# Reloads for a weight check moved to unit 80 and after, and a planner's order made anew with other task times

## The chip, the cores and the metric

One NeuronCore of a Trainium2 chip runs the whole kernel. The metric is the device time of one execution in microseconds; less is better. PE is TensorE's matmul, PEld its weight load, DVE VectorE, ACT ScalarE, POOL GpSimd, SP the engine that here only issues DMAs. A trailing q marks an engine's sequencer.

## What is computed

A decayed linear attention over 4 x 8 heads of 768 steps, and then a gated two-layer block over its 3072 rows of 384 numbers:

```python
for t in range(S):
    state = alpha[:, :, t, :, None] * state + einsum('bhd,bhe->bhde', k[:, :, t], v[:, :, t])
    y[:, :, t] = einsum('bhd,bhde->bhe', q[:, :, t], state)
h = x @ w_in                       # x: y as 3072 rows of 384; w_in 384 x 2048, float64
sp = where(h > 20, h, log1p(exp(min(h, 20))))
return ((h * tanh(sp)) @ w_out)    # w_out 2048 x 384, float64
```

## The kernel before

**Pieces of work.** The attention is cut into 24 chunks (`attention(n)`), each 64 steps of one pair of batches. The gated block is cut into units (`unit`): `SEGMENTS` lists 105 of them, each a slice of 128 of the 2048 inner columns (f = 0 to 15) for 2 or 4 chunks of 128 rows. The weights are 16 slices of 768 KB (`weight(f)`).

**A weight slice** is loaded by SP into one of two `stage` buffers (L426), taken apart by four DVE operations through the one `lead` buffer (L441, L447, L453, and L468, which stands on PE and ACT for f < 3) and one ACT copy (L459). The units' matmuls read the two halves in `wio`.

**A chunk** costs DVE two scans (L570, L583), a reciprocal, two products (L579, L593), a decay (L601), two masks (L650), and later a state update (L800) and the lower halves of x (L699). PE turns k (L761), makes scores (L616 and L639) and y with the change of state (L616, L680). Six small DMAs of x (`move`, L720) then go out on SP; the chunk's units can begin when they have landed. Three `qka` buffers hold loaded chunks.

**A unit** is nine matmuls up into one of two `h` banks (L826), then ACT exp, square, log, exp; a DVE gate (L847); an ACT copy (L853); a DVE lower half (L856); and three matmuls down for each of its chunks (L885). Sums of up to four chunks stay in banks o0 to o3 over many units; chunks 0 to 3 and 4 to 7 use the same four. So units 24 to 33 (chunks 0 to 3, f = 6 to 15) have to end before a down of units 34 to 40 (chunks 4 to 7, f = 9 to 15) can begin. `EARLY_BANKS` says which banks a chunk uses; without an entry it is "att" thrice.

**The check.** Each weight slice is loaded a second time (`weight_check`, L497) into a `stage` buffer, and one DVE operation (L506 or L508) gathers its exponents in `unlike`; `weights_checked` (L519, L520) looks at them. At the end flags are summed (L1003), every engine loads the result (L1141) and branches (L1142): `general_path` is the other arm, not run with these inputs. In the arm that runs, SP goes over the counters of its DMA queues that the other arm would have advanced.

**What sets the order.** The program for each engine is a fixed list. `Plan.order` makes it while the kernel is built: every task has an engine, a cost (`COST`: time on the engine, time until its result), needs, buffers, and a key. Of each engine's tasks it takes the one that can begin first by these costs, and among those that can begin at once the one with the lowest key. The chip then follows the lists at its own pace, with semaphores. Keys count units:
- unit i: i + SHIFT; its downs have that + 3 (`LAG`).
- chunk n: due + SHIFT. Due is 8 units before its first unit (`LEAD`), and at least 2 before the next chunk's due. Scores have + 0.2, y + 0.5, the six moves + 0.64, the load - 6.
- weight f: first unit with f, less 4 (`W_LEAD`), + SHIFT; its load has 4 less.
- check f: `CHECK_FROM` + f x `CHECK_STEP` + SHIFT; its load has 4 less and comes behind the up of one unit (`behind`, a condition for the planner alone).

Where by these costs PE would have nothing to do in the first 130 us, the planner puts in fills (L940): matmuls of a constant into a free bank, whose result nobody reads.

Of the kernel before, what the change touches and what calls it, by code (L numbers as in the profile page):

```python
# [27 lines left out]
B, H, S, D = 4, 8, 768, 48  # L28
DM, FF = 384, 2048
P = 128  # L30
# [4 lines left out]
NFF = FF // P  # L35
NK = DM // P
# [26 lines left out]
FIRST_W = -6.0  # L63
CHECK_FROM = 57.0
CHECK_STEP = 2.7
COLD = 14
# [3 lines left out]
EARLY_BANKS = {  # L70
    0: "o1 o1 att o3 att".split(),
    1: "att o3 o1 att h".split(),
    2: "att h att att o3".split(),
    3: "o0 h att o0 o3".split(),
    4: "o2 att o3".split(),
    9: "o3 att o2".split(),
    10: "o1 o3 att".split(),
    11: "o3 o1 att".split(),
    13: "o1 o2 att".split(),
    14: "att o0 o1".split(),  # L80
    15: "o3 att att".split(),
    16: "att att o1".split(),
    17: "o2 o3 att".split(),
    18: "o3 att o0".split(),
    20: "att o3 o2".split(),
    21: "att att h".split(),
    22: "att o2 att".split(),
}
SHIFT = {
    "chunk": {  # L90
# [4 lines left out]
    },  # L95
    "unit": {
# [17 lines left out]
    },  # L114
    "weight": {
        0: -1.8297, 1: -88.668, 2: -1.298, 3: -0.44909, 4: -0.76088, 5: -0.16277, 7: -7.1065,
        8: -3.6601, 9: -2.0214, 11: 0.91205, 12: -0.61512, 13: 2.8687, 15: 3.8897,
    },
    "weight check": {
        1: 2.9506, 2: -1.2413, 3: -2.7653, 4: -7.2029, 5: -0.37293, 6: -5.1126, 7: -4.9684,  # L120
        8: -0.99544, 9: -8.3869, 10: -8.6038, 11: 6.855, 12: 3.149, 13: -24.555, 14: 0.49888,
        15: 1.0013,
    },
# [26 lines left out]
class Plan:  # L150
# [14 lines left out]
    def add(  # L165
        self, engine, cost, late, key, emit, needs=(), uses=(), behind=(), port=False,
        small=(False, False),
    ):
        t = Task(engine, cost, late, key, emit, port)
        t.small = small  # L170
        t.needs, t.uses, t.behind = list(needs), list(uses), list(behind)
        for u in t.uses:
            u.left += 1
            u.key = min(u.key, key)
        self.tasks.append(t)
        return t
# [107 lines left out]
WINDOW = 10**6  # L284
SAME = 0.155
QUEUE = 8
# [6 lines left out]
    "cold fill": (0.32, 0.36), "fill": (0.1635, 0.2), "off": (0.21, 0.37), "w off": (0.88, 1.06),  # L293
    "w seen": (1.4, 1.6),
    "scan": (1.152, 1.27), "inverse": (0.113, 0.21), "mult k": (0.562, 0.745), "mult": (0.602, 0.725), "half mult": (0.32, 0.46), "check": (0.2, 0.34),
    "state": (0.272, 0.4), "state0": (0.21, 0.35), "decay": (0.469, 0.605), "mask": (0.335, 0.49),
    "scores0": (0.65, 0.77), "scores": (0.91, 1.0), "y0": (1.12, 1.2), "y": (1.36, 1.43),
    "y last": (0.88, 0.99), "turn": (0.34, 0.66),
# [12 lines left out]
for _n in (1, 2):  # L311
    COST["lead", _n] = (0.095 + 0.2 * _n, 0.17 + 0.2 * _n)
    COST["bits", _n] = (0.114 + 0.401 * _n, 0.2 + 0.4 * _n)
    COST["w left", _n] = (0.069 + 0.401 * _n, 0.185 + 0.4 * _n)
    COST["w hi", _n] = (0.095 + 0.32 * _n, 0.21 + 0.32 * _n)
# [4 lines left out]
def fast_path(ctx, tc, qka, v, w, out, good):  # L320
    nc = tc.nc
# [15 lines left out]
    for rows in (slice(0, HALF), slice(HALF, P)):  # L337
        nc.gpsimd.affine_select(
            out=causal_f[rows], in_=one[rows, :HALF], pattern=[[1, HALF]], compare_op=ALU.is_ge,
# [151 lines left out]
    def weight_check(f):  # L491
# [19 lines left out]

        t = add("SP", *COST["load w"], key - 4, load, uses=[again], behind=[ups[int(key)]])
        seen.append(
# [493 lines left out]
def general_path(ctx, tc, q, k, v, alpha, w_in, w_out, out):  # L1007
# [9 lines left out]
    with tc.tile_pool(name="rec", bufs=1) as sb:  # L1017
# [4 lines left out]
        with tc.For_i(0, S, T) as t0:  # L1022
            qt, kt, vt, at = [sb.tile([BH, T, D], F32, name=n) for n in ("qt", "kt", "vt", "at")]
            yt = sb.tile([BH, T, D], F32, name="yt")
            for dst, src in zip((qt, kt, vt, at), flat):
                nc.sync.dma_start(dst, src[:, ds(t0, T), :])
            for t in range(T):
# [7 lines left out]
            for b in range(B):  # L1035
                dst = x_d[b * S : (b + 1) * S, :].rearrange("t (h e) -> h t e", h=H)
                nc.sync.dma_start(dst[:, ds(t0, T), :], yt[b * H : (b + 1) * H])

    with tc.tile_pool(name="conv", bufs=1) as sb:
# [5 lines left out]
        with tc.For_i(0, DM * FF // P, W) as c0:  # L1045
            t = sb.tile([P, 2, W, 2], I32, name="words")
            for m in range(2):
                nc.sync.dma_start(
                    t[:, m].rearrange("p c w -> p (c w)"), words[m][:, ds(c0 * 2, 2 * W)]
                )  # L1050
# [21 lines left out]
            for m in range(2):  # L1072
                nc.sync.dma_start(w_d[m][:, ds(c0, W)], f[:, m])

    with tc.tile_pool(name="moe", bufs=1) as sb, tc.tile_pool(name="pm", bufs=1, space=PSUM) as ps:
# [6 lines left out]
        as_rows = lambda t, n: t.rearrange("p c -> (p c)").rearrange("(s r c) -> r s c", s=n, r=P)  # L1082
        nc.sync.dma_start(wi, as_rows(w_d[0], NK))
        nc.sync.dma_start(wo, as_rows(w_d[1], NFF))
        with tc.For_i(0, B * S, P) as r0:
            x = sb.tile([P, DM], F32, name="x_g")
            nc.sync.dma_start(x, x_d[ds(r0, P), :])
            xT = sb.tile([P, NK, P], F32, name="xT_g")
# [27 lines left out]
            nc.scalar.copy(o, po)  # L1116
            nc.sync.dma_start(out[ds(r0, P), :], o)

# [91 lines left out]
```

## Time and profile before

| | us |
|---|---|
| time, median of 3 runs (480.13 to 480.57) | 480.56 |
| time of the profiled execution | 480.47 |
| its span, first to last instruction | 478.8 |
| around the span | 1.67 |
| PE busy in it, of which fills | 466.8, of which 17.5 |
| DVE busy, ACT busy | 340.9, 365.6 |
[...]

A row of a timeline is: start and length in us, engine, line, operation, written tile and read tiles, their shapes, how often; in brackets the idle time of the engine just before, and what ended it. "issue" there means that the engine waited for nothing that the profile shows. A matmul's length includes its way through the array, so one begins before the last has ended: the pace of a group is read from its start to the start of the next group. DMA shares are of 16 DMA engines; a row of DMA issues ends with the KB of one and the median us from issue to landing, a row of a queue has packets, MB and share. Packets of the kind "instruction" bring the engines' own programs.

### The profile page before, as it was taken

Reading aid. Unit: us, or ns where it says so; the run is one execution under the profiler, and the core shown is the slowest. Engines: PE = TensorE matmul, PEld = TensorE weight load, DVE = VectorE, ACT = ScalarE, POOL = GpSimd, SP = SyncE. Lnnn points to the kernel's source line nnn. Section 1 sums busy time; section 2 is a strip of 40 time slices with the busy share of each in tenths; the row PEclk is TensorE's granted clock in tenths of the full one; section 3 lists DMA queues with packets and bytes.
Section 4 is the critical chain, followed back from the end, with each engine's and each line's share of the span. In section 5 each row is a group of like instructions: output and inputs, shape, how many; then the busy total and the mean of one; then the engine's idle time right before and its main releaser. Section 6 shows DMA issues by size and latency. Waiting matters only on the chain.

```text
span 478.8 us, 12662 instructions
## 1 busy us (share of the span) xinstructions
PE 466.8 (97%) x5233; PEld 418.6 (87%) x5233; DVE 340.9 (71%) x586; ACT 365.6 (76%) x816; POOL 2.4 (1%) x12
## 2 busy tenths in 40 slices
PE   7999999999999999999999989999999999999996
PEld 4668888998989889999999978999989989999995
DVE  8999999999995799789434368797376343355432
ACT  2567879889998968877887846878758878778784
POOL 2000000000000000000000000000000000000000
PEclk9999999999999999999999999999999999999998
DMA  8777536353220363154000266824252000080001
GB/s 292 247 235 253 178 127 231 135 168 115 66 67 9 129 197 111 67 184 159 0 1 0 77 223 213 318 68 132 63 183 81 1 7 4 22 291 18 0 2 70
DMA packets 20078, 56.82 MB, mean 119 GB/s; under 512 B 4016, under 2 KB 12464, under 8 KB 20016
## 3 DMA queue, kind: packets, MB, share of 16 engines
q1 hardware_dynamic: 19872, 55.77, 33.9%
q8 instruction: 42, 0.69, 0.6%
q10 hardware_dynamic: 144, 0.20, 0.1%
q14 instruction: 20, 0.16, 0.1%
HBM read 48.87 MB, written 4.72 MB: 112 GB/s over the span
## 4 chain that ended last, share of the span: by engine, by line
PE 74%; DVE 16%; ACT 6%; issue 2%; DVEq 0%
PE bank L826 31%; PE bank L885 31%; PE bank L616 4%; PE bank L940 2%; DVE t L847 2%; PE bank L639 2%; DVE rest L570 2%; PE bank L761 2%; PE bank L680 2%; DVE g L856 1%; DVE qka L583 1%; DVE w_lead L453 1%; DVE w_lead L447 1%; DVE wio L468 1%; DVE state L800 1%
## 5 line engine op out<-in xcount | busy, mean ns | idle before, releaser
L885 PE MATMUL bank<-wio,g 128*128 128x384 f32 x1152 | 207.4, 329 | 0.0
L826 PE MATMUL bank<-xs,wio 128*128 128x512 f32 (+1 forms) x945 | 205.3, 364 | 1.1 <-DVE t L847 0.8
L885 PEld LDWEIGHTS bank<-wio,g 128*128 128x128 f32 x1152 | 189.8, 189 | 5.0 <-issue 0.2
L826 PEld LDWEIGHTS bank<-xs,wio 128*128 128x128 f32 x945 | 164.0, 189 | 22.1 <-DVE t L847 3.1
L856 DVE SCALAR_TENSOR_TENSOR g<-t,g 128x512 fp32r<-128x512 f32 (+1 forms) x105 | 66.3, 642 | 55.7 <-ACT g L853 55.5
L847 DVE SCALAR_TENSOR_TENSOR t<-t,bank 128x512 f32<-128x512 f32 (+1 forms) x105 | 67.0, 638 | 48.0 <-ACT t L844 47.7
L835 ACT ACTIVATE t<-bank 128x512 f32<-128x512 f32 (+1 forms) x105 | 58.8, 560 | 48.6 <-PE bank L826 45.5
L853 ACT ACTIVATE g<-t 128x512 fp32r<-128x512 f32 (+1 forms) x105 | 60.5, 586 | 20.7 <-DVE t L847 10.6
L841 ACT ACTIVATE t<-t,fifth 128x512 f32<-128x512 f32 (+1 forms) x105 | 71.7, 684 | 2.2
L838 ACT ACTIVATE t<-t 128x512 f32<-128x512 f32 (+1 forms) x105 | 62.0, 592 | 2.1
L844 ACT ACTIVATE t<-t 128x512 f32<-128x512 f32 (+1 forms) x105 | 61.7, 588 | 1.5
L570 DVE TENSOR_TENSOR_SCAN rest<-qka,behind 112x520 f32<-112x520 f32 x24 | 29.7, 1238 | 1.3 <-DMA qka<-in_qka_dram 1.1
L583 DVE TENSOR_TENSOR_SCAN qka<-qka,ahead 112x520 f32<-112x520 f32 x24 | 29.6, 1232 | 0.0
L694 ACT ACTIVATE xs<-bank 112x256 fp32r<-112x256 f32 x48 | 15.8, 379 | 14.8 <-PE bank L680 6.9
L650 DVE COPY_PREDICATED probs<-causal,bank 128x256 f32<-128x256 uint32 x48 | 18.8, 439 | 6.8 <-PE bank L639 5.7
L835 ACT ACTIVATION_READ_ACCUMULATOR t<-bank 128x1 f32 x105 | 20.5, 195 | 0.0
L616 PE MATMUL bank<-qka,state 48*48 48x64 f32 (+1 forms) x704 | 20.0, 221 | 0.3 <-DVE qka L593 0.2
L800 DVE TENSOR_TENSOR state<-bank,state 112x192 f32<-112x192 f32 x40 | 12.9, 353 | 10.3 <-PE bank L680 6.4
L616 PEld LDWEIGHTS bank<-probs,v 64*48 64x48 f32 (+1 forms) x768 | 13.6, 127 | 7.4 <-issue 3.4
L940 PE MATMUL bank<-behind 112*128 112x384 bf16 x76 | 17.5, 367 | 2.4 <-DVE behind L362 2.4
L616 PEld LDWEIGHTS bank<-qka,state 48*48 48x48 f32 (+1 forms) x704 | 15.3, 127 | 4.8 <-issue 3.1
L508 DVE SCALAR_TENSOR_TENSOR unlike<-wc,unlike 128x768 int32<-128x768 int32 x15 | 17.0, 1134 | 3.0 <-DMA wc<-in_wp_dram 3.0
(70 smaller groups left out, 316.6 us busy)
## 6 DMA issues: line engine op xcount, KB each, us to landing
qka<-in_qka_dram SPq DMA_DIRECT2D x22, 772.5 KB, 6.0
ws<-in_wp_dram SPq DMA_DIRECT2D x16, 768.0 KB, 4.4
wc<-in_wp_dram SPq DMA_DIRECT2D x16, 768.0 KB, 5.0
v<-in_vp_dram SPq DMA_DIRECT2D x24, 192.0 KB, 3.2
out_dram<-osb SPq DMA_DIRECT2D x15, 192.0 KB, 2.3
xs<-xs SPq DMA_DIRECT2D x144, 16.0 KB, 3.6
out_dram<-part SPq DMA_DIRECT2D x8, 192.0 KB, 2.5
qka<-in_qka_dram SPq DMA_DIRECT2D x2, 260.5 KB, 3.8
```

Source lines behind the costliest of these rows:

```text
L570: nc.vector.tensor_tensor_scan(t[:, :0:-1], alpha()[:, :0:-1], behind[:, ::-1], 0.0, ALU.mult, ALU.max)
L583: nc.vector.tensor_tensor_scan(a, a, ahead, 0.0, ALU.mult, ALU.max)
L616: return nc.tensor.matmul(summed(x)[HALF * side : HALF * side + wide, j], weights(wide), moving, start=start, stop=stop, skip_group_check= ...
L826: nc.tensor.matmul(p[:, :N], wio[:, z, f, 0, s * P : s * P + P], by_token(x[:, s, :, a]), start=m == 0, stop=m == len(passes) - 1,)
L835: nc.scalar.activation(wide(t), wide(h), AF.Exp, accum_out=uchk[:, at : at + 1])
L838: nc.scalar.activation(wide(t), wide(t), AF.Square, bias=1.0)
L841: nc.scalar.activation(wide(t), wide(t), AF.Ln, bias=fifth, scale=0.2)
L844: nc.scalar.activation(wide(t), wide(t), AF.Exp, scale=-1.0)
L847: nc.vector.scalar_tensor_tensor(wide(t), wide(t), 2.5, wide(h), ALU.subtract, ALU.mult)
L853: nc.scalar.activation(g.tile[:, 0, :N], wide(t), AF.Copy, scale=-0.4)
L856: late[mybir.EngineType.DVE] = nc.vector.scalar_tensor_tensor(g.tile[:, 1, :N], wide(t), -0.4, g.tile[:, 0, :N].bitcast(F32), ALU.mult, AL ...
L885: made = nc.tensor.matmul(o.tile[:, :DM], g.tile[:, a, j * C : (j + 1) * C], spread(wio[:, z, f, 1]), start=begins and m == 0, stop=end an ...
```

## The change

Reloads and checks have their keys from 80 on in steps of 1.05 and no shifts, and each reload comes behind the up of the unit that `CHECK_FROM` + f x `CHECK_STEP` names. All shifts of chunks, units and weights and all early banks are new. Some task times of the planner are new, and `SAME`, by which the planner lets small matmuls follow small ones earlier. In `general_path` all DMAs go from SP's queue to POOL's. No operation on data in the arm that runs is added, removed or resized.

```diff
-CHECK_FROM = 57.0
-CHECK_STEP = 2.7
+CHECK_FROM = 80.0
+CHECK_STEP = 1.05
...
 EARLY_BANKS = {
-    0: "o1 o1 att o3 att".split(),
...
-    16: "att att o1".split(),
-    17: "o2 o3 att".split(),
-    18: "o3 att o0".split(),
-    20: "att o3 o2".split(),
-    21: "att att h".split(),
-    22: "att o2 att".split(),
+    0: "att att o0 att o1".split(),
...
+    17: "o0 att att".split(),
+    18: "o1 o3 o2".split(),
+    19: "o1 att att".split(),
+    21: "att o3 o2".split(),
 }
 SHIFT = {
     "chunk": {
-        0: -15.485, 1: -12.079, 2: -11.416, 3: -11.777, 4: -0.33581, 5: 1.6274, 6: -0.39491,
-        7: 1.5292, 8: -3.7056, 9: -0.21255, 10: 1.4965, 11: -0.0097693, 12: -8.9524, 13: -7.0071,
-        14: -7.7326, 15: -9.7059, 16: -9.893, 17: -7.5153, 18: -6.1157, 19: -3.0825, 20: -3.4548,
-        21: -3.5097, 22: -5.4473, 23: 2.0482,
+        0: -25.301, 1: -20.34, 2: -13.806, 3: -11.23, 4: 4.0517, 5: 4.0522, 6: 1.3752,
+        7: 0.80117, 8: -3.6406, 10: -0.2315, 11: 1.4964, 12: -2.1029, 13: -3.5335, 14: -4.1898,
+        15: -1.3139, 16: -11.016, 17: -10.764, 18: -8.744, 19: -5.913, 20: 0.29965, 21: 0.71137,
+        22: 0.22851, 23: 4.8182,
     },
     "unit": {
...
-        85: -1.3119, 86: -0.71045, 87: -3.9605, 88: 0.03174, 89: -0.96161, 90: -4.4882,
...
-        104: -0.55339,
...
+        79: 2.1935, 80: 0.049234, 81: 1.4386, 82: 0.13712, 83: -0.18346, 85: 1.6807, 86: 0.44438,
+        87: 0.29401, 89: -0.3835, 90: 0.76619, 91: -0.44769, 92: 0.71218, 93: -0.79337,
...
+        100: -0.91033, 101: 0.41587, 102: -0.2893, 104: 11.602,
     },
     "weight": {
-        0: -1.8297, 1: -88.668, 2: -1.298, 3: -0.44909, 4: -0.76088, 5: -0.16277, 7: -7.1065,
-        8: -3.6601, 9: -2.0214, 11: 0.91205, 12: -0.61512, 13: 2.8687, 15: 3.8897,
+        0: 0.44719, 1: -53.48, 2: -19.485, 3: -0.79106, 4: 2.6882, 5: -2.1876, 6: -2.2027,
+        7: 4.5643, 8: 4.1694, 9: 0.97864, 10: -1.3843, 11: -0.13355, 12: -2.0257, 13: -0.16652,
+        14: 6.07, 15: 10.996,
     },
     "weight check": {
-        1: 2.9506, 2: -1.2413, 3: -2.7653, 4: -7.2029, 5: -0.37293, 6: -5.1126, 7: -4.9684,
-        8: -0.99544, 9: -8.3869, 10: -8.6038, 11: 6.855, 12: 3.149, 13: -24.555, 14: 0.49888,
-        15: 1.0013,
+
     },
 }
...
-SAME = 0.155
+SAME = 0.33
...
-    "w seen": (1.4, 1.6),
+    "w seen": (1.6, 1.8),
...
-    "scores0": (0.65, 0.77), "scores": (0.91, 1.0), "y0": (1.12, 1.2), "y": (1.36, 1.43),
+    "scores0": (0.65, 0.77), "scores": (0.91, 1.0), "y0": (1.12, 1.2), "y": (1.39, 1.46),
...
-    COST["lead", _n] = (0.095 + 0.2 * _n, 0.17 + 0.2 * _n)
-    COST["bits", _n] = (0.114 + 0.401 * _n, 0.2 + 0.4 * _n)
+    COST["lead", _n] = (0.095 + 0.24 * _n, 0.17 + 0.24 * _n)
+    COST["bits", _n] = (0.114 + 0.435 * _n, 0.2 + 0.435 * _n)
...
-        t = add("SP", *COST["load w"], key - 4, load, uses=[again], behind=[ups[int(key)]])
+        t = add("SP", *COST["load w"], key - 4, load, uses=[again], behind=[ups[int(CHECK_FROM + f * CHECK_STEP)]])
...
-                nc.sync.dma_start(dst, src[:, ds(t0, T), :])
+                nc.gpsimd.dma_start(dst, src[:, ds(t0, T), :])
...
```

## Rows read from the trace of the kernel before

**Rows 1.** The page: busy us (share of span) and instructions of TensorE, VectorE, ScalarE
```profile
PE 466.8 (97%) x5233; PEld 418.6 (87%) x5233; DVE 340.9 (71%) x586; ACT 365.6 (76%) x816; POOL 2.4 (1%) x12
```
**Rows 2.** Stages: length, then busy us (count) by engine, granted clock, DMA share, GB/s
```profile
60.00:146.00 86.00, 85.08 (x849) 77.25 (x848) 85.28 (x139) 74.61 (x180) 0.00 (x0) 1.00 0.37 126
146.00:268.00 122.00, 121.76 (x1476) 111.59 (x1476) 83.27 (x150) 95.82 (x207) 0.00 (x0) 1.00 0.25 84
268.00:300.00 32.00, 29.72 (x624) 26.05 (x623) 21.25 (x43) 20.41 (x50) 0.00 (x0) 1.00 0.56 201
```
**Rows 3.** The group of fills (page), and DVE alone from its first scan on
```profile
L940 PE MATMUL bank<-behind 112*128 112x384 bf16 x76 | 17.5, 367 | 2.4 <-DVE behind L362 2.4
...
3.68:145.59 141.91, 139.59 (x232) 1.00 0.51 175
```
**Rows 4.** Timelines of DVE and PE where weight slice 15 is finished
```profile
145.59 0.96 DVE L468 TENSOR_TENSOR wio<-w_lead,wio 128x768 fp32r<-128x768 f32 x1 [0.32 <-ACT wio L459]
...
145.97 4.37 PE L826 MATMUL bank<-xs,wio 128*128 128x512 f32 x18
```
**Rows 5.** Timeline of PE at its longest wait; the page's queue of PE's instruction packets
```profile
283.92 0.26 PE L616 MATMUL bank<-probs,v 64*48 64x64 f32 x2 [1.48 <-issue]
...
q8 instruction: 42, 0.69, 0.6%
```
**Rows 6.** DMA in 268 to 278, in 278.5 to 281.5, in 281.5 to 284
```profile
wc<-in_wp_dram SPq DMA_DIRECT2D x2, 768.0 KB, 7.5
...
q1 hardware_dynamic: 221, 1.21, 98.6%
xs<-xs SPq DMA_DIRECT2D x5, 16.0 KB, 5.4
...
q8 instruction: 1, 0.02, 2.4%
```
**Rows 7.** Timeline of PE, 288 to 297: two waits for DVE
```profile
289.00 0.60 PE L761 MATMUL bank<-ident,qka 112*128 112x112 f32 x4 [0.56 <-DVE qka L579]
...
295.26 0.69 PE L616 MATMUL bank<-probs,v 64*48 64x64 f32 x32 [0.21 <-DVE probs L650]
...
296.57 1.24 PE L885 MATMUL bank<-wio,g 128*128 128x384 f32 x6
```
**Rows 8.** The tile wc: ns min/median/max, first and last start
```profile
L508 DVE SCALAR_TENSOR_TENSOR unlike<-wc,unlike x15: 945/1143/1218, 281.0 to 440.7; 128x768 int32<-128x768 int32 x15
```
**Rows 9.** Timeline of PE: attention among units; chunk 23's y and what follows
```profile
161.79 0.69 PE L616 MATMUL bank<-probs,v 64*48 64x64 f32 x32
...
163.82 2.21 PE L826 MATMUL bank<-xs,wio 128*128 128x512 f32 x9
...
385.98 0.46 PE L616 MATMUL bank<-qka,state 48*48 48x64 f32 x16
...
386.83 2.21 PE L826 MATMUL bank<-xs,wio 128*128 128x512 f32 x9
388.97 0.69 PE L616 MATMUL bank<-probs,v 64*48 64x64 f32 x32
...
403.56 2.11 PE L826 MATMUL bank<-xs,wio 128*128 128x512 f32 x9
405.51 2.11 PE L885 MATMUL bank<-wio,g 128*128 128x384 f32 x12
```
**Rows 10.** The tile xs from 384 to 404: chunk 23's six moves and their landing
```profile
L720 SPq DMA_DIRECT2D xs<-xs x6: 507/580/597, 392.1 to 395.4; - x6
...
DMA to landing us min/median/max: 1.8/1.8/2.3
```
**Rows 11.** Timeline of the last units: downs after the last up, and the last DVE operation
```profile
465.84 7.96 PE L885 MATMUL bank<-wio,g 128*128 128x384 f32 x48
...
470.74 0.69 DVE L856 SCALAR_TENSOR_TENSOR g<-t,g 128x512 fp32r<-128x512 f32 x1 [0.76 <-ACT g L853]
```
**Rows 12.** Line 1142, SP's counters after the branch: ns, first and last start
```profile
L1142 SPq EVENT_SEMAPHORE  x8: 17/17/17, 476.4 to 477.4; - x8
```

More of the change, by code (lines that the diff above doesn't have):

```diff
@@ L70 @@
 EARLY_BANKS = {
-    0: "o1 o1 att o3 att".split(),
[L72 to L81, printed above, removed]
-    16: "att att o1".split(),
-    17: "o2 o3 att".split(),
-    18: "o3 att o0".split(),
-    20: "att o3 o2".split(),
-    21: "att att h".split(),
-    22: "att o2 att".split(),
+    0: "att att o0 att o1".split(),
+    1: "o1 h o1 o0 o3".split(),
+    2: "att o3 o0 att h".split(),
+    3: "att o1 att o3 o0".split(),
+    4: "o3 att att".split(),
+    5: "o3 att att".split(),
+    9: "o1 att att".split(),
+    10: "att o3 o2".split(),
+    11: "o3 att att".split(),
+    12: "o2 att o3".split(),
+    13: "att o2 o0".split(),
+    14: "h att att".split(),
+    17: "o0 att att".split(),
+    18: "o1 o3 o2".split(),
+    19: "o1 att att".split(),
+    21: "att o3 o2".split(),
 }
@@ L1036, in general_path @@
                 dst = x_d[b * S : (b + 1) * S, :].rearrange("t (h e) -> h t e", h=H)
-                nc.sync.dma_start(dst[:, ds(t0, T), :], yt[b * H : (b + 1) * H])
+                nc.gpsimd.dma_start(dst[:, ds(t0, T), :], yt[b * H : (b + 1) * H])
     with tc.tile_pool(name="conv", bufs=1) as sb:
@@ L1047, in general_path @@
             for m in range(2):
-                nc.sync.dma_start(
+                nc.gpsimd.dma_start(
                     t[:, m].rearrange("p c w -> p (c w)"), words[m][:, ds(c0 * 2, 2 * W)]
@@ L1072, in general_path @@
             for m in range(2):
-                nc.sync.dma_start(w_d[m][:, ds(c0, W)], f[:, m])
+                nc.gpsimd.dma_start(w_d[m][:, ds(c0, W)], f[:, m])
     with tc.tile_pool(name="moe", bufs=1) as sb, tc.tile_pool(name="pm", bufs=1, space=PSUM) as ps:
@@ L1082, in general_path @@
         as_rows = lambda t, n: t.rearrange("p c -> (p c)").rearrange("(s r c) -> r s c", s=n, r=P)
-        nc.sync.dma_start(wi, as_rows(w_d[0], NK))
-        nc.sync.dma_start(wo, as_rows(w_d[1], NFF))
+        nc.gpsimd.dma_start(wi, as_rows(w_d[0], NK))
+        nc.gpsimd.dma_start(wo, as_rows(w_d[1], NFF))
         with tc.For_i(0, B * S, P) as r0:
             x = sb.tile([P, DM], F32, name="x_g")
-            nc.sync.dma_start(x, x_d[ds(r0, P), :])
+            nc.gpsimd.dma_start(x, x_d[ds(r0, P), :])
             xT = sb.tile([P, NK, P], F32, name="xT_g")
@@ L1116, in general_path @@
             nc.scalar.copy(o, po)
-            nc.sync.dma_start(out[ds(r0, P), :], o)
+            nc.gpsimd.dma_start(out[ds(r0, P), :], o)
 @with_exitstack
```

27 rows, old and new, of the table SHIFT are left out of this document.

## The prediction

> **What bounds the kernel now.** I read the page first: TensorE is busy for 97% of the span [rows 1], so at first sight PE is the bound and only its idle time and its fills can be won. The fills alone take 17.5 us [rows 3]. The table by stage, read next, corrects this. From 60 to 146 us DVE is busy for 85.28 of 86.00 us, and only after 146 does it have room (83.27 of 122.00) while PE has none (121.76) [rows 2]. For DVE alone from its first scan at 3.68 to 145.59 the row says 139.59 busy of 141.91 us, so 2.32 idle [rows 3]. The timelines show where the one bound hands over to the other: DVE begins the last operation on weight slice 15 at 145.59, and PE begins the up of unit 33, the first reader of that slice, at 145.97 [rows 4]. So there are two stages: DVE sets the pace up to 146, PE from there to the end. The fills are the shadow of DVE's stage; they are not won by giving PE other work unless DVE comes to slice 15 sooner.
>
> After 146, PE's losses are few. The timeline has one wait of 1.48 us in the midst of chunk 18's y, ended by nothing that the profile shows ("issue") [rows 5], and two for DVE, 0.56 and 0.21 us, both in chunk 19 [rows 7]. The stage table agrees: from 268 to 300 PE is busy for 29.72 of 32.00 us, where from 146 to 268 it lacks only 0.24 [rows 2].
>
> What was the 1.48 us? The queue q8 brought 42 packets and 0.69 MB, 16 KB a packet [rows 5]. PE had 5233 weight loads and 5233 matmuls [rows 1], some 249 a packet: these are its instruction blocks. Two reloads were issued between 268 and 278 and took 7.5 us to land; from 278.5 to 281.5 the DMA engines were 98.6% taken by q1, the data, and no q8 packet moved; one came between 281.5 and 284 [rows 6], and PE went on at 283.92 [rows 5]. Chunk attention burns instructions: a y with the next chunk's scores begins at 161.79 and is over at 163.82 [rows 9], 128 matmuls in 2.03 us by their count there. I take the wait for one for a block that stood behind loads, the two reloads among them: the first check of their line ran at 281.0 [rows 8].
>
> **The change, part by part.** I start from the profiled execution's own 480.47 us; the median of the runs is 0.09 above.
>
> *Start, to 146.* The work that DVE must do before unit 33 doesn't change: slices 0 to 15, chunks 0 to 8, the units' gates, and the scans of chunks 9 to 11, for their new keys (29.0, 30.8, 34.5: due 29, 31, 33 plus shift) stay below that of slice 15, which goes from 32.9 to 40.0 (unit 33, less 4, plus 10.996). Slices 3 and 5 come before chunk 4 now (1.2 and 1.8 against 3.05), which gives PE the four-chunk units 6 to 8 sooner and may save fills, but what PE gains there it waits for at unit 33. At best DVE's 2.32 us of idle time go [rows 3]. At worst slice 15, whose key now lies behind those of the gates of units 31 to 38, lets two more gates of 0.7 us pass: 1.4 us more. I take 0.3 us won, near the nothing that a full DVE allows.
>
> *The wait for a block.* The reloads go from units 57 and up to unit 80 and up, where no chunk but the last is in work. In the rows their checks ran from 281.0 to 440.7 [rows 8]; now they leave the stretch where chunks 16 to 19 are loaded. Bounds: all 1.48 us won, or as much lost again where chunk work under the new order meets loads once more. I take 1.2 won, since two reloads of 768 KB no longer share that stretch with the chunk loads.
>
> *The two waits for DVE.* A check of 1.14 us [rows 8] stood among chunk 19's operations at 288.86 and its load shared the DMA engines with the chunk's. Without them 0.77 us go at best; at worst as much appears elsewhere. I take 0.5 won. Checks themselves cost nothing at their new place: after unit 80 DVE has two operations per unit, 0.69 us each [rows 11], of 3.9 us (an up and four downs), so 16 checks of 1.14 us hide there; without that cover they would be 18 us.
>
> *Grouping.* Alone, scores take 0.85 us (385.98 to 386.83), y 1.31 us (295.26 to 296.57) [rows 7, 9]; together 2.03, so 0.13 less. An up that is followed by y takes 2.14 us to the next start, one followed by a down 1.95 [rows 9], so a group spares 0.19 more: 0.32 us for each two that are joined. After 146 there are 15 chunks. With four more joined or parted it is 1.3 us either way. New banks let chunks 16, 20, 22 and 23 use "att" alone, which parts some; `SAME` lets others meet. I take nothing.
>
> *The end.* Unit 104's key is 115.6 now, behind all downs that are ready. In the rows 48 matmuls of downs follow its up without a break from 465.84, at 0.1625 us from start to start. The last 12 are its own, so 36 cover its way through ACT and DVE: 465.84 + 36 x 0.1625 is 471.69, and its last DVE operation ends at 470.74 + 0.69 = 471.43 [rows 11]. With 12 of them before the up instead, 12 x 0.1625 - 0.26 = 1.7 us would be bare. That needs a unit's downs to be ready when PE turns to that up, which the rows don't settle: I take nothing and keep 1.7 for the range. Of the DMAs that go to POOL none is run. SP's eight counters after the branch lie from 476.4 to 477.4 [rows 12]; some may go to POOL, beside them: nothing to 0.4 won, or as much lost on POOL; I take 0.2 won.
>
> *Sum:* 480.47 - 0.3 - 1.2 - 0.5 - 0.2 = 478.27, with the 0.09 between the profiled time and the median 478.4.
>
> [...]
>
> **The rivals.**
>
> *A. Nothing to win.* DVE stays the bound to 146 at the same time, and the 1.48 us were not the reload's, or come again at another pair of chunks: other blocks are fetched during chunk loads too, and four chunks in a row remain. For it: DVE's idle time is under 2% of its stage. Against it: the packet, the full DMA engines and the wait lie in one line. Then 0.5 + 0.2 remain of the sum, 480.56 - 0.7 = 479.9; it decides if PE's waits after 146 again add up to 2 us. The same 479.9 comes out if the 1.48 us were no fetch at all. [...]
>
> *B. The last chunk comes late: slower.* Chunk 23's key goes from 83.05 to 85.82. Its y (key 86.3) then stands after the up of unit 84, and the first unit that reads it has 88.6 (unit 89). Between them by key are the ups of units 85 to 88 and the downs of unit 84, 5 x 1.95 = 9.75 us. In the rows y begins at 388.97, the last move is issued at 395.4 and lands 1.8 us later [rows 9, 10]: 8.2 us. Before, the queue was empty there. Now the reloads of units 80 to 96 are in the same queue of SP and in the same DMA engines: in a full stretch a move took 5.4 us [rows 6], which makes 11.8, 2.0 us short, and a reload ahead of the moves that waits for a stage buffer until a check is done adds some of the 7.5 us that a reload took; with 5 of them it is 7.0 short. Downs of units 85 and 86 (3.9 us) can be drawn forward, but then the next up's way of 5.6 us [rows 11] finds only one more up and its own two banks before it, 1.7 us bare. So 7.0 - 3.9 + 1.7 = 4.8 us, 483.2. It decides when x of chunk 23 lands more than 9.75 us after y's start. Against it: the planner knows of the moves' time and may draw the reloads apart, and DVE has room.
>
> **How the numbers follow.** The forecast has 0.60 (its own range 476.0 to 479.5), A 0.22, B 0.13, and 0.05 for a worse start or end. A measurement of this kernel can tell about 0.2%, 0.96 us, from no change, so faster means under 479.6, slower over 481.5. The forecast gives 0.60 faster; A gives 0.22 the same; B and the rest 0.18 slower. All lower ends together (2.32 + 1.48 + 0.77 + 1.3 + 0.4) would give 474.3; that all meet is unlikely, so I go to 475.6. Above, A is held whole and the milder half of B: 481.8.
>
> **What would show it.** Right: unit 33's up within 2 us of 146; PE full from there to the end but for under 1 us of waits; no "issue" wait over 0.5 us in chunks 16 to 19; checks on DVE from about 370 us on; a gapless end. A shows as a wait of 1 us or more among chunk matmuls with the DMA engines full. B shows as PE idle before the first up after chunk 23's y, released by a DMA of xs. I would be wrong altogether if unit 33's up came more than 3 us earlier, for then DVE's first stage was not the wall that I take it for.

## The result and the profile after

The kernel after takes 475.75 us (median of 7 runs, 475.59 to 478.78), the kernel before beside it 480.41 us (7 runs): ratio 0.9904, 95% interval 0.9885 to 0.9923. In two later sessions the kernel after came to 475.90 and 476.01 us where before took 481.46 both times (0.9884 and 0.9889). So it is faster by 4.7 to 5.6 us. The forecast was 478.4, a gain of 2.2 us: the sign and the range of 475.6 to 481.8 held, the size was less than half of what came.

The profiled execution of after takes 476.18 us, its span 474.7; before's was 480.47 and 478.8. First the page of the kernel after, its row of busy times and its fills (columns as in [rows 1] and [rows 3]):

```profile
PE 465.2 (98%) x5239; PEld 419.3 (88%) x5239; DVE 340.4 (72%) x586; ACT 363.5 (77%) x816; POOL 2.4 (1%) x12
...
L936 PE MATMUL bank<-behind 112*128 112x384 bf16 x82 | 18.7, 360 | 2.6 <-DVE behind L358 2.6
```

Then its three stages, to be held against [rows 2]:

```profile
60.00:146.00 86.00, 85.04 (x854) 78.31 (x854) 85.07 (x139) 77.66 (x188) 0.00 (x0) 1.00 0.36 122
146.00:268.00 122.00, 121.04 (x1630) 110.09 (x1630) 87.52 (x160) 92.29 (x203) 0.00 (x0) 1.00 0.27 87
268.00:300.00 32.00, 32.00 (x484) 29.35 (x483) 25.12 (x47) 25.80 (x59) 0.00 (x0) 1.00 0.39 129
```

Last, all that TensorE waited for, whole span (us in total, times, longest):

```profile
PE bank L936 <- DVE behind L358: 2.6, 1, 2.6
PE bank L881 <- DVE g L852: 1.0, 1, 1.0
PE bank L612 <- DVE probs L646: 0.9, 1, 0.9
PE pf L999 <- DVE every L985: 0.9, 1, 0.9
PE bank L612 <- issue: 0.2, 1, 0.2
```

The third stage is the plainest: PE is busy for 32.00 of 32.00 us there, before for 29.72 [rows 2], and the waits of [rows 5] and [rows 7] have no counterpart. The fills didn't shrink (82, 18.7 us, against 76 and 17.5 in [rows 3]), and VectorE is as full up to 146 us as it was (85.07 of 86.00 us; 85.28 in [rows 2]). One would say that the start gained nothing. It gained a large part of what the forecast missed, and the group of downs up to 150 us shows it; first before, then after, first and last start behind the durations:

```profile
L885 PE MATMUL bank<-wio,g x264: 326/326/463, 37.2 to 145.8; 128*128 128x384 f32 x132
```
```profile
L881 PE MATMUL bank<-wio,g x276: 326/326/462, 38.6 to 147.9; 128*128 128x384 f32 x138
```

The ups begun by then are as many in both (315 matmuls), and so is the chunks' work; after has 12 matmuls of downs more, 12 x 0.1625 = 1.95 us of work that PE has behind it.

Against before this lead is not kept all the way. The same group up to 260 us and up to 300 us, each time before and then after:

```profile
L885 PE MATMUL bank<-wio,g x543: 326/326/463, 37.2 to 260.0; 128*128 128x384 f32 x181
L881 PE MATMUL bank<-wio,g x531: 326/326/462, 38.6 to 257.8; 128*128 128x384 f32 x177
...
L885 PE MATMUL bank<-wio,g x621: 326/326/463, 37.2 to 299.9; 128*128 128x384 f32 x156
L881 PE MATMUL bank<-wio,g x636: 326/326/462, 38.6 to 298.5; 128*128 128x384 f32 x159
```

At 260 us both have begun 522 matmuls of ups. After is 12 matmuls of downs behind (1.95 us) and a chunk's scores and y ahead (2.03 us in [rows 9]), so the two are about level. At 300 us their chunk work is equal, and after is ahead by 15 matmuls of downs and 7 of ups, 15 x 0.1625 + 7 x 0.2165 = 3.95 us (nine matmuls of an up take 1.95 us from start to start in [rows 9]). So after's order gives the lead back between 180 and 260 us, 0.96 us of it in the wait at 183 us that is shown further down, and wins some 4 us between 260 and 300, more than the 2.25 us of before's three waits there.

### The profile page after: what moved, and what is told of

It is laid out like the page before. It is cut to its first block, busy times and chain, and to the rows that moved or that the text cites. A ratio compares the mean times of both kernels' runs of the same rounds, so it can differ in the third digit from the quotient of the medians.

```text
span 474.7 us, 12675 instructions
## 1 busy us (share of the span) xinstructions
PE 465.2 (98%) x5239; PEld 419.3 (88%) x5239; DVE 340.4 (72%) x586; ACT 363.5 (77%) x816; POOL 2.4 (1%) x12
## 4 chain that ended last, share of the span: by engine, by line
PE 91%; DVE 5%; DMA 2%; issue 1%; SPq 1%; ACT 0%; DVEq 0%
PE bank L822 38%; PE bank L881 38%; PE bank L612 5%; PE bank L936 2%; PE bank L635 2%; PE bank L676 2%; PE bank L757 2%; DMA qka<-in_qka_dram 1%; DVE rest L566 1%; DMA xs<-xs 1%; SPq L716 1%; DVE qka L579 0%; PE bank L474 0%; DVE t L843 0%; DVE w_lead L443 0%
## 5 line engine op out<-in xcount | busy, mean ns | idle before, releaser
L881 PE MATMUL bank<-wio,g 128*128 128x384 f32 x1152 | 203.9, 328 | 1.0 <-DVE g L852 1.0
L936 PE MATMUL bank<-behind 112*128 112x384 bf16 x82 | 18.7, 360 | 2.6 <-DVE behind L358 2.6
```

The costliest lines, as they stand in the source:

```text
L881: made = nc.tensor.matmul(o.tile[:, :DM], g.tile[:, a, j * C : (j + 1) * C], spread(wio[:, z, f, 1]), start=begins and m == 0, stop=end an ...
```

## The experiments

Most of them change nothing but the order. The planner's result is replaced by a written list of its task numbers, so that a task can be put elsewhere with its instructions untouched:

```diff
-    tasks = plan.order()
+    fills, tasks = 0, []
+    for entry in ORDER:
+        if isinstance(entry, int):
+            tasks.append(plan.tasks[entry])
+        else:
+            tasks.append(plan.fill(plan.tasks[entry[0]].uses[entry[1]], fills))
+            fills += 1
```

"Ahead by x us" in the expectations means: the matmuls begun up to a time, each at its undisturbed distance from start to start, compared between two traces. Every run is given with the median of before beside it on the same chip; the medians of before were 480.41, 480.93, 481.25, 481.46 and 481.46 us in five sessions.

### The reloads alone, and the cut of the order in two

**Late reloads in before's order.**

```diff
 up 56
-load wc0
...
 up 80
+load wc0
...
 up 83
+load wc1
```

> The kernel before with one thing changed: the 16 reloads for the weights' check and the DVE steps that read them stand where the kernel after has them (first reload behind the 80th up, last behind the 96th), all else in before's order. Theory (the reloads among the last chunks' loads filled the DMA queues and starved TensorE's instruction fetch): the 1.48 us without a releaser at 283.92 and the two DVE waits of 0.56 and 0.21 us at 289 to 296 go, 480.4 - 2.25 = 478.2 us, and 478.9 if only the first goes. Rival A (another wait takes their place): 479.7 to 480.4. Rival B (the reloads now stand ahead of chunk 23 or of the last hand-overs): 481.5 or more.

Measured: 484.35 us, before 480.93, ratio 1.0064 (1.0039 to 1.0089). The time is in rival B's range. The trace shows both halves: the wait of 1.48 us is gone, and VectorE, which takes its list in order, stands 2.96 and 1.84 us for reloads in front of unit gates, near the moves of chunk 23 that rival B named. Its timeline, and what PE waited for behind 260 us:

```profile
397.02 1.18 DVE L629 SCALAR_TENSOR_TENSOR unlike<-wc,unlike 128x768 int32<-128x768 int32 x1 [2.96 <-DMA wc<-in_wp_dram]
400.04 0.96 DVE L629 SCALAR_TENSOR_TENSOR unlike<-wc,unlike 128x768 int32<-128x768 int32 x1 [1.84 <-DMA wc<-in_wp_dram]
...
PE bank L947 <- DVE t L968: 3.4, 1, 3.4
PE pf L1130 <- DVE every L1116: 0.9, 1, 0.9
PE bank L882 <- DVE qka L700: 0.5, 1, 0.5
PE bank L737 <- DVE probs L771: 0.2, 1, 0.2
```

The two DVE waits of [rows 7] are still there (the third and fourth waits), with no reload near them: they are not the reloads' doing.

How the wait of 1.48 us went is seen in the DMA rows from 278.5 to 281.5 us, where before's queue of data took 98.6% and PE got no packet of instructions [rows 6]. With the reloads late:

```profile
q1 hardware_dynamic: 212, 0.27, 26.0%
q8 instruction: 1, 0.02, 1.8%
```

PE's packet lands at 280.39 us here. In before it lands at 282.52, and PE goes on 1.40 us later. Six waits of this kind in five traces agree (before, the spaced reloads, the part of the change that stands further down, and the two cuts that keep before's order behind them): in each PE goes on 1.34 to 1.57 us after a packet has landed.

**Late and evenly spaced.** The same, with one load about every 1.2 ups and its VectorE step 29 entries behind it.

> The kernel before with the reloads and their DVE steps late again, but evenly spaced by hand (the first behind the 78th up, one about every 1.2 ups, each DVE step some 29 entries behind its load where the late placing of the first try had 10 to 23). In that first try the wait without a releaser at 282 us was gone (TensorE 1.7 us ahead of before at 290 us), and 3.54 us were lost at 398.6 us, where VectorE stood 2.96 and 1.84 us waiting for reloads that SyncE had issued at 392.5 and 393.6 us. Theory (the reloads cost TensorE only where its instruction fetch, or a DVE step ahead of a gate, waits for them): 480.4 - 1.7 = 478.7 us on a chip where before takes 480.4 (ratio 0.9965). Rival (late reloads cost by the bytes that they add beside chunk 23's hand-overs, wherever they stand): again 1.01 or more.

Measured: 479.24 us, before 481.25, ratio 0.9949 (0.9929 to 0.9969): 2.0 us won by the reloads' place alone. PE's waits from 260 to 470 us:

```profile
PE bank L737 <- issue: 0.7, 2, 0.4
PE bank L882 <- DVE qka L700: 0.6, 1, 0.6
PE bank L737 <- DVE probs L771: 0.2, 1, 0.2
```

The wait for a block has shrunk to two of 0.4 us at most, and was zero in the first try: the reloads were its larger part. The gain is more than the 1.48 us. One source of the rest is seen: in one profiled run before's order also loses time to a reload that its own VectorE step waits for. The next row is from it, the run with one part of the change that stands further down, which is before's order unchanged, and there PE lost 0.87 us right behind it. That this makes up the whole difference is not shown. The row:

```profile
365.33 1.11 DVE L508 SCALAR_TENSOR_TENSOR unlike<-wc,unlike 128x768 int32<-128x768 int32 x1 [0.99 <-DMA wc<-in_wp_dram]
```

**Early reloads in after's order.** The first diff the other way round, in after.

> The kernel after with one thing changed back: the 16 reloads and their DVE steps stand after as many ups as in the kernel before (first behind the 56th up), all else in after's order. Theory (the reloads make the instruction wait wherever they meet the last chunks' loads): a wait of 1 to 1.5 us without a releaser comes back between 260 and 300 us, and up to 0.8 us of DVE waits: 475.75 + 1.5 to 2.25 = 477.3 to 478.0. Rival (the wait went because chunks 12, 15 and 16 are spread further apart in after, and the reloads were innocent): 475.8, no such wait.

Measured: 487.31 us, before 480.93, ratio 1.0129 (1.0103 to 1.0154), some 11 us over after. Both theories fell. No wait without a releaser came back; what came is again VectorE's order. Its timeline, then PE's waits behind 150 us:

```profile
289.30 0.96 DVE L626 SCALAR_TENSOR_TENSOR unlike<-wc,unlike 128x768 int32<-128x768 int32 x1 [3.84 <-DMA wc<-in_wp_dram]
290.18 0.68 DVE L974 SCALAR_TENSOR_TENSOR g<-t,g 128x512 fp32r<-128x512 f32 x1
...
PE bank L1003 <- DVE g L974: 6.4, 4, 3.8
PE bank L944 <- DVE t L965: 1.4, 2, 1.2
```

The operation at 290.18 is a unit's lower half, its last product on VectorE. Its input was there at 284.5 us, and it stood behind the reload's step, for whose load VectorE waited 3.84 us. After's order and early reloads don't go together; why the reloads came so late there is not shown.

**After's start, before's rest (cut at 150 us).**

```diff
+(after's first 830 entries)
+(before's entries without those, in before's order)
```

> After's order for the first 830 entries (to about 150 us, chunks 0 to 8 with after's banks), then before's order for all that is left, its early reloads included. If the 2.08 us by which after's TensorE has done more work at 150 us are worth their face: 480.4 - 2.1 = 478.3 (477.8 to 478.8). If the dense part takes them back (the loads of chunks 12 to 19 are paced by the DMA engines, so TensorE waits there for what it gained): 479.7 or more.

Measured: 482.20 us, before 480.93, ratio 1.0025 (1.0005 to 1.0045). PE is 2.15 us ahead at the cut and loses 1.46 us of it within 5 us behind the cut, where before's units stand too close together to go on from after's state; 1.5 us more go at a late reload:

```profile
365.29 1.00 DVE L631 SCALAR_TENSOR_TENSOR unlike<-wc,unlike 128x768 int32<-128x768 int32 x1 [1.76 <-DMA wc<-in_wp_dram]
```

In before's profile the same step began at 363.34 without a wait for a load. Since the cut itself costs, this run doesn't tell what the start is worth.

**The same, cut at 180 us.**

> After's order for its first 995 entries (to about 180 us, where its TensorE had done 2.74 us more work than before's), then before's order for the rest, early reloads included. With the cut at 150 us TensorE was 2.15 us ahead at the cut and lost 1.46 us within 5 us behind it, at an exp-to-gate chain of ScalarE that stood too close behind its up. Theory (that loss came from the cut, and the start's gain carries): 0.3 to 1.5 us ahead of before at 280 us and 478.9 to 480.0 where before takes 480.4. Rival (before's dense part has its own limit, chunk loads or ScalarE, and takes back whatever the start won): level with before at 270 us, 480.4 or more.

Measured: 486.21 us, before 481.25, ratio 1.0091 (1.0071 to 1.0112). Inconclusive too: from 180 to 196 us PE waits 2.9 us for a gate and 1.9 us for chunk work, right behind the cut. After's start was not joined to before's rest without a loss, so this direction stays open.

**Before's start, after's rest (cut at 152 us).**

> The converse: before's order for its first 845 entries (to about 152 us), then after's order for all that is left. If the start is worth 2.1 us and the rest with the tail the other 2.2 to 2.6: 475.75 + 2.1 = 477.85 (477.3 to 478.4). If the start counts for nothing: 475.8 to 476.3. If the rest counts for nothing without the new start: 479.7 or more.

Measured: 481.64 us, before 480.93, ratio 1.0007 (0.9988 to 1.0025). By its waits this kernel should have been at 479: 2.8 us stood at its very end, where no engine works. VectorE's last instructions in the program's branch, in this run and in after (duration, first and last start):

```profile
L1264 DVEq COMPARE_BRANCH  x1: 84/84/84, 474.9 to 474.9; - x1
L1264 DVEq EVENT_SEMAPHORE  x1: 21/21/21, 479.2 to 479.2; - x1
```
```profile
L1138 DVEq COMPARE_BRANCH  x1: 84/84/84, 472.2 to 472.2; - x1
L1138 DVEq EVENT_SEMAPHORE  x1: 21/21/21, 472.8 to 472.8; - x1
```

**The same with a shorter program for VectorE.**

```diff
+(before's first 845 entries)
+(after's entries without those, in after's order)
...
-                nc.gpsimd.dma_start(dst, src[:, ds(t0, T), :])
+                nc.sync.dma_start(dst, src[:, ds(t0, T), :])
```

> Before's start to 152 us and after's rest, as in the run before, but the eight DMAs of the path that never runs are on SyncE's queue again, which makes VectorE's program 825 instructions long in place of 837. In the run before, VectorE's first instruction behind its branch at the end came 4.16 us after the branch where it takes 0.53 in the other kernels. Theory (that is the fetch of the branch's target, and depends on where the program's end lies): the gap is 0.5 us again, the end costs 3.7 us from the last verdict, and the time is 481.64 - 2.8 + 0.27 = 479.1 where before takes 480.9 (ratio 0.996); the 2.1 us between that and after's ratio of 0.9904 (2.7 us) are the start. Rival (the gap is a chance of that one profile): the time stays at 481.6 to 481.9.

Measured: 478.14 us, before 481.25, ratio 0.9924 (0.9905 to 0.9944). The gap behind the branch is back at 0.53 us. This is the cut that holds: nothing breaks at it. PE's only waits from 260 to the end are those of the last verdict, so the two DVE waits of [rows 7], 0.8 us in the spaced reloads, went with after's order of the chunks. The 1.1 us between 478.14 and the spaced reloads' 479.24 on the same chip are the worth of all of after's order behind 152 us: by the count of matmuls this kernel is 1.3 us behind the spaced reloads at 260 us and 1.0 ahead at 300, so they are a balance, and not those two waits alone. What this kernel lacks against after is the start: at 150 us it has begun 266 matmuls of downs where after has 276.

### Where the start wins

**Two more cuts.** As the last one, at 92 and at 118 us, and the kernel after beside them.

> Before's order for its first 575 entries (to about 92 us), after's from there, the DMAs of the path that never runs on SyncE's queue. With the cut at 152 us the ratio was 0.9924, after's is 0.9884 to 0.9904 and SyncE's queue costs 0.0006. Theory (most of the start's gain is made behind 92 us, where before's TensorE loses some 0.2 to 0.5 us at each of five gates and after's loses 0.4 us in all): only 0.4 us of the gain is missing, ratio 0.990 to 0.992. Rival (it is made ahead of 92 us, by the fills and the first chunks): as with the cut at 152 us, 0.992 to 0.994.

Measured: 483.79 us, before 481.46, ratio 1.0047 (1.003 to 1.0065). Inconclusive: this cut breaks a chain, PE waits 5.22 us for a unit's lower half at 100.15.

> Before's order for its first 697 entries (to about 118 us), after's from there, SyncE's queue as above. By the two traces after is 1.33 us ahead at 120 us and 2.08 at 150. Theory (the gates between 92 and 118 us and slice 15's wall share the gain): 1.3 us of it is missing, ratio 0.991 to 0.993, between the cuts at 92 and 152 us. Rival (slice 15's wall alone makes it): as after, 0.989 to 0.991.

Measured: 477.76 us, before 481.46, ratio 0.9921 (0.99 to 0.9942).

> The kernel after itself beside the two cuts: ratio 0.988 to 0.991.

Measured: 476.01 us, before 481.46, ratio 0.9889 (0.9863 to 0.9914). The run before it, for the session of the next experiments:

> The kernel after itself, to stand beside the runs that follow on the same chip. From the first comparison: ratio 0.9904 (0.9885 to 0.9923); two runs with the same code agree within 0.4%, so 0.988 to 0.993.

Measured: 475.90 us, before 481.46, ratio 0.9884 (0.9859 to 0.9908). With before's order up to 118 us, 1.75 us are lost against after on the same chip, 0.26 of them at the end (below). By the trace PE is 1.0 us behind after at 118 us and stays 1.0 us behind to the end; with the cut at 152 us it is 1.6 us behind at 150 and 1.9 at the end. So in front of after's rest the start's gain is real and lasts to the end, and some 1.0 us of it is made ahead of 118 us. One execution is a thin base for this, but the others agree: counted at 118 us against before's own profile, the seven profiles that begin with before's order stand at -0.8 to 0.3 us (median 0.0), the nine that begin with after's at -0.1 to 1.6 (median 1.25). The times alone can't part the two cuts (0.9921 and 0.9924). The waits don't tell how it is won. From 60 to 150 us they come to 0.8 us in before, to 0.6 in the cut at 118, and to 0.9 in after, there for a chunk's mask:

```profile
PE bank L826 <- DVE t L847: 0.8, 3, 0.4
```
```profile
PE bank L942 <- DVE t L963: 0.6, 2, 0.4
```
```profile
PE bank L612 <- DVE probs L646: 0.9, 1, 0.9
```

**Unit 35 behind the wall.**

```diff
-up 35
 up 32
 up 33
+up 35
 up 34
```

> The kernel after with one unit moved: unit 35's up, its ScalarE and VectorE chain, stand behind unit 33's up (unit 34's and 36's shift one place) instead of ahead of unit 32's, so that TensorE comes to unit 33, which needs weight slice 15, with nothing of the next group of rows done ahead. Theory (slice 15's last conversion is a wall that after only passes because 1.9 us of unit 35's up fill the time in front of it): a wait of 0.7 to 1.5 us for VectorE in front of unit 33's up near 146 us and 476.5 to 477.3 where after takes 475.75 (ratio 0.992 to 0.994). Rival (the order of the units has nothing to do with it; the work in front of slice 15 is simply done sooner): no such wait, 475.8 (0.9904).

Measured: 478.05 us, before 481.25, ratio 0.9925 (0.9905 to 0.9945): 1.0 to 2.0 us slower than after, whose ratios were 0.9884 to 0.9904. VectorE's last operation on slice 15, and the up of unit 33 that waits for it:

```profile
145.89 0.96 DVE L586 TENSOR_TENSOR wio<-w_lead,wio 128x768 fp32r<-128x768 f32 x1 [0.92 <-ACT wio L577]
...
146.91 1.78 PE L944 MATMUL bank<-xs,wio 128*128 128x512 f32 x7 [0.29 <-DVE wio L586]
...
160.31 0.92 PE L944 MATMUL bank<-xs,wio 128*128 128x512 f32 x3 [0.45 <-DVE t L965]
```

The place is the theory's and the ratio is in its 0.992 to 0.994, though it counts a loss near 410 us that has nothing to do with the slice. The wait at the slice is smaller than its 0.7 (0.29 us by the row, 0.46 from start to start), and by 180 us 1.1 more are lost at the gates of the next units, which now come closer together (one of them in the third row). That other loss is some 0.6 us at a single gate, which unit 35's place doesn't explain. Now the kernel after at the same place:

```profile
147.21 0.96 DVE L464 TENSOR_TENSOR wio<-w_lead,wio 128x768 fp32r<-128x768 f32 x1 [0.56 <-ACT wio L455]
...
140.26 4.11 PE L822 MATMUL bank<-xs,wio 128*128 128x512 f32 x18
144.21 4.06 PE L881 MATMUL bank<-wio,g 128*128 128x384 f32 x24
148.11 1.24 PE L822 MATMUL bank<-xs,wio 128*128 128x512 f32 x5
```

The 18 matmuls from 140.26 are the ups of units 35 and 32, the 24 behind them downs of units 30 and 31, and unit 33 follows at 148.11 without a wait. Slice 15 came 1.6 us later than in [rows 4], unit 33 2.1 us later, and PE was none the worse: it had done the up of a unit of the next rows, and the downs of unit 31, which before does behind unit 33.

### The end of the program, and one repair

**One part of the change.**

```diff
-                nc.sync.dma_start(dst, src[:, ds(t0, T), :])
+                nc.gpsimd.dma_start(dst, src[:, ds(t0, T), :])
```

> The kernel before with one part of the change: the eight DMAs of the path that never runs are issued by GpSimd. The runs so far fall in two groups by this part alone: from the last verdict to the end 3.70 to 3.72 us with SyncE's queue, 3.43 to 3.45 with GpSimd's. Theory: 3.43 to 3.45 here, everything in front of it as before: 0.27 us less (ratio 0.9994). Rival (one more queue to set up or wait for costs what the counters save): 3.7 or more, ratio 1.000 or above.

Measured: 481.73 us, before 481.46, ratio 1.0006 (0.9988 to 1.0024). The end is 3.42 us from the last verdict where before has 3.70, so 0.28 us are won there; the time of the whole kernel is too uncertain to show so little.

**Four instructions that never run.**

```diff
         nc.vector.memset(st, 0.0)
+        nc.vector.memset(st, 0.0)
+        nc.vector.memset(st, 0.0)
+        nc.vector.memset(st, 0.0)
+        nc.vector.memset(st, 0.0)
```

> The kernel after with four more VectorE instructions in the path that never runs, so that VectorE's program is 837 instructions long, as where the branch's target was reached after 4.16 us; after has 833. No instruction that runs is added or moved. Theory (the target then lies in code that has not been fetched at the branch): VectorE's first instruction behind the branch comes about 4.2 us behind it in place of 0.53, and the kernel takes 2.8 us more (475.75 to 478.5, ratio 0.996). Rival (the length isn't what decides; in the other kernel it was the number of executed instructions in front of the branch): 0.53 us, 475.75 (0.9904).

Measured: 478.74 us, before 481.46, ratio 0.9939 (0.9918 to 0.9961); after in the same session 475.90. So 2.84 us are lost, and VectorE's rows say where:

```profile
L1142 DVEq COMPARE_BRANCH  x1: 84/84/84, 472.8 to 472.8; - x1
L1142 DVEq EVENT_SEMAPHORE  x1: 21/21/21, 477.0 to 477.0; - x1
```

**A repair at 182 us.**

```diff
-gate of unit 39
 last product of unit 38
+gate of unit 39
-second scan of the chunk
 last product of unit 39
+second scan of the chunk
```

> The kernel after with two VectorE steps in another order near 182 us: unit 38's last multiplication stands ahead of unit 39's gate, and chunk's second scan behind unit 39's last multiplication. In after TensorE waits there 0.96 us for unit 38's multiplication, which VectorE takes up behind unit 39's gate though its input is there 0.3 us before. Theory: the wait shrinks to 0.3 us, TensorE is 0.6 us ahead at 190 us and stays so: 475.2 (ratio 0.989). Rival (unit 39 comes later by as much, or the dense part further on gives the gain back): 475.75 or more.

Measured: 475.89 us, before 481.46, ratio 0.9888 (0.9865 to 0.9911), no faster than after in the same session. (A last product is the unit's lower half.) After's profile has the first of the next rows; with the repair the downs run through from 180.81.

```profile
183.24 1.08 PE L881 MATMUL bank<-wio,g 128*128 128x384 f32 x5 [0.96 <-DVE g L852]
```
```profile
180.81 5.36 PE L1003 MATMUL bank<-wio,g 128*128 128x384 f32 x27
```

The wait is gone and the time is not. In after's own profile of the same session the loss at this place was 0.37 us in place of the first one's 1.12 (from start to start), so there was less to win than the single profile said.

## Why the prediction was right or wrong

Set against the runs, the terms of the sum are:

| term | forecast | measured | by |
|---|---|---|---|
| start, to 146 | 0.3 | 0.7 to 1.9 | cut at 152 us against after: 0.7 to 1.7 by the ratios less the end, 1.9 by the traces |
| wait for a block, reloads | 1.2 | 2.0 | spaced reloads against before |
| two DVE waits | 0.5 | 1.1 for all of the order behind 152 us | cut at 152 us against spaced reloads |
| the end | 0.2 | 0.25 to 0.28 | from the last verdict to the end |

They add to 4.1 to 5.3 us, and after is 4.7 to 5.6 us faster. This is no check of the terms: each is the step from one kernel to the next on the way from before to after, so they have to add up to about the whole.

- **The start was the term most mis-sized,** 0.3 us against 0.7 to 1.9. The step that failed reads "what PE gains there it waits for at unit 33". The reading of [rows 2] and [rows 3] was right: VectorE is full to 146 us in both kernels, and slice 15 came no sooner, even 1.6 us later. The wall is there too, as the run with unit 35 behind it shows. But a wall holds only the work that needs it. Unit 35, of the next rows, needs slice 10 alone, and the ups and downs done ahead of unit 33 were taken as fixed where the new order changes them. The bound of 2.32 us from VectorE's idle time was a bound on slice 15, not on PE. The sentence on being wrong altogether asked for unit 33 to come 3 us earlier; it came 2.1 us later, and the start won all the same: the time of one event was the wrong thing to watch. The number of PE's matmuls done by then was a better one, though no promise, since the order behind it can give a lead back, as after's did by 260 us.
- **The wait for a block** was read rightly: with the reloads gone from that stretch the packet came 2.1 us earlier, and the wait went to 0 in one run and to two of 0.4 us at most in another. The term was too small by 0.8 us, at least in part by what [rows 8] hide: a step of VectorE that waits for its reload holds the gates behind it (waits of 2.96 and 1.84 us with the late reloads, and 3.4 us of PE's for the gate behind them). Before's order paid 0.87 us of this in one profiled run, and the kernel with early reloads in after's order, which does it most, is 11 us slower than after. That risk was named only for chunk 23's moves.
- **The two DVE waits** went, but not for the reason given. The reloads' step at 288.86 had no part in them: they stand unchanged in both runs that take the reloads away from there, and go with after's order of the chunks. A right sign from a wrong cause.
- **The end** is as taken: the last downs run without a gap, nothing of the 1.7 us at unit 104 came, and 0.25 to 0.28 us go behind the last verdict. **Grouping** was taken as nothing, and no run takes it apart from the rest of the order.
- **The other blocks,** of which rival A says that they are fetched during chunk loads too, show no such wait in after: with as many packets, 42, its trace has none over 0.2 us, before's the one of 1.48. From 278.5 to 281.5 us the data take 35.8% of the DMA engines in after and 98.6% in before, so in these two traces the long wait stands in the stretch that the data filled.
- **Rival A** falls with the waits that went, **rival B** with the trace: chunk 23's y stands at 383.2 us, the first unit that reads it at 402.1, without a wait. Its mechanism, a reload in the way, is real all the same, in the two runs that lost by moving the reloads, though there VectorE's step waited for the load and not chunk 23.

What stays open: how the order ahead of 118 us wins its 1.0 us (the cut at 92 us, which should tell, broke a chain), where after's order loses its lead between 180 and 260 us beyond the one wait of 0.96, and why two executions of one kernel differ by up to 1 us in their first 100 us.

## What to carry to other kernels

A full engine says when its last product comes, not how far the others are by then: count in each order what the engine that sets the pace next has done at the hand-over, and ask which work there doesn't need the late product. A load that nothing urgent reads still stopped what stood behind its reader on VectorE, which takes its list in order (waits of 2.96 us with the late reloads, 3.84 with the early ones in after's order), so a background transfer needs slack in its reader's place as well as a free queue. And a wait is only tied to a cause when it goes as that cause alone is taken away: of the waits that the trace seemed to lay at the reloads' door, the one for a block was theirs for the larger part, and the two for VectorE were not.

## What the runs showed of the hardware

Code that never runs cost time here: with four more VectorE instructions in the path behind the branch (837 in its program in place of 833), the first instruction behind the branch came 4.14 us after it in place of 0.53, and the kernel took 2.84 us more. A second kernel with 837 showed the same 4.16 us, and those with 798 to 833 did not. The queue of instruction packets of 8 KB, from about 1 us ahead of the branch to the end, has one more in the slow kernel; this run first, then after:

```profile
q14 instruction: 5, 0.04, 2.2%
```
```profile
q14 instruction: 4, 0.03, 3.3%
```

The one more began at 477.58 us, behind VectorE's first instruction at 476.99, and the four ahead of it had landed by 474.95. So from 833 to 837 instructions, with nothing changed that runs, the gap went from 0.53 to 4.14 us. What VectorE waited for in it was not shown: the fetch of the branch's target that two of the expectations name is the author's guess, and no row here shows it.

A reload's way varied: in before one of 768 KB, issued at 358.7 us, had landed by 363.3; in the cut at 150 us, which has before's order from there on, it was issued at 358.6 and came at 365.3, and VectorE stood 1.76 us for it.
